# A gated hedgehog attention kernel: where the casts of the weight tails, one early weight split and four early stores stand in their engines' queues

## The chip, the cores and the metric

One core of a Trainium2 chip runs the whole kernel. Its engines work from queues of their own, each strictly in order: TensorE (PE, with its weight loads PEld), VectorE (DVE), ScalarE (ACT), GpSimd (POOL) and SyncE (SP), which here only issues transfers. Engines wait for one another, and for transfers, through semaphores. The metric is the time of one execution on the device, in microseconds (us).

## The reference

One row block of x (2048 rows, 576 columns, float32) goes through two branches whose results are joined:

```
xn = layernorm(x)
q, k, v = split of xn @ wqkv into 32 heads of 18
phi(t)  = [softmax(t @ w_phi), softmax(-t @ w_phi)]       for q and k, per head
o       = phi(q) (phi(k)^T v) / (phi(q) (phi(k)^T 1) + 1e-6)
s       = o @ wo
g       = silu( (silu(xn @ w_gate) * (xn @ w_up)) @ w_down )      4608 hidden columns
result  = x + s * g
```

## The kernel before

All products are float32-exact to a few bits by splitting each operand into a rounded part ("hi", type fp32r) and a rest ("lo"): ACT casts hi, DVE (or GpSimd) subtracts to get lo, and PE sums three products. So each operand costs one cast and one subtraction before PE can use it.

The work comes in five stages. *Preparation* (to about 70 us): x is loaded, normalised and transposed into eight blocks XB, and w_phi is folded into the weights of k and q. *Keys* (to about 230 us): sixteen key tiles of 128 rows, their softmaxes, and the sum kv = phi(k)^T v. *Queries* (to about 490 us): sixteen query tiles (`q_tile`), in pairs, with the numerator (`numer`) and the projection with wo (`project`) of the pair before. *Gate and up*, with *down*: 36 hidden blocks f of 128 columns in two row halves i, by a Strassen-like scheme that saves products. An end that joins the branches.

Five of the 36 hidden blocks, the early ones (`EARLY = 5`), are computed ahead, plainly, in the first three stages, as filling for PE: `early_weights(f)` (line 100) loads two raw weight pieces on SP's queue and splits each (`split_rows`: ACT's cast at line 62, DVE's subtractions at lines 63 and 64); `early_tile(f, i, parts)` (line 113) computes gate and up for two column groups of 512 rows, with a SiLU on ACT (line 119), a product on DVE (line 123), and a store of h to DRAM on SP's queue (line 124). The tiles of h have two buffers, and the two PSUM banks `pe` are shared by gate and up: the next gate product needs the SiLU of the one before to be done. The first two early blocks are done for the half i = 1 in the preparation (line 262); f = 1 and f = 0 are finished and f = 2, 3 done in the query stage (lines 645 to 648); f = 4 stands between the stages.

`tails(n)` (line 544) prepares, for four of the other hidden blocks at a time, the last 32 + 32 rows of the weights: a load on SP's queue (line 547), four subtractions on GpSimd (549 to 552), a cast on ACT (tile `th`, line 553), a subtraction on DVE (line 554), and twelve stores to DRAM issued by GpSimd (line 557): eight of the cast, four of the rest. There are eight of them, and the main stage reads what they store.

`softmax_parts` (line 275) is the part of a key or query tile behind its product: a maximum and a minimum over each head on DVE (line 280), two subtractions that read PSUM (line 281, kept in the list `read`, two a tile), two exponentials on ACT (line 284, the last of them kept in `exps`), and a sum. `q_tile` goes on with products on DVE, the last of which (line 580) is kept in `last_e`. There is one PSUM tile for the query product, so the next query tile's product (`p L92`) waits for the second subtraction of the tile before.

A planner lays out each engine's order: it takes instructions by their place in the program as they become ready by its own estimates, ahead of others where the code says `high_priority`. `tc.issue_after(ins)` binds it: what the block issues on the engine of `ins` stands behind `ins` in that engine's queue; instructions on other engines are not bound. So with `last_e[...]` around `tails(n)` (line 642), only the DVE subtraction of the tail is bound.

Of the kernel before, what the change touches and what calls it, by code (L numbers as in the profile page):

```python
# [18 lines left out]
NT = S // P  # L19
BT = 512  # L20
# [26 lines left out]
def gated_hedgehog_kernel(ctx: ExitStack, tc, x, w_qk, w_v, w_phi, wo, w_gu, w_tail, w_down, ident_in, mask_in, out):  # L47
# [5 lines left out]
    nc = tc.nc  # L53
# [7 lines left out]
    def split_rows(hi, lo, src):  # L61
        nc.scalar.copy(hi, src)
        nc.vector.tensor_sub(lo, src[:, :, 0:2], hi[:, :, 0:2])
        nc.vector.tensor_sub(hi[64:96, :, 2], src[64:96, :, 2], hi[64:96, :, 2])
# [6 lines left out]
    h_dram = dram.tile([2, EARLY, P, HS], F32, name="h_dram")  # L71
# [10 lines left out]
    def xw(ps, i, j, cols, wh, wl, stationary_x):  # L82
        pairs = []
        for k in range(2):
            b = XB[i][2 * j + k]
            for c in range(2):
                pairs += [(b[:, c, cols], w[:, k, c]) for w in (wh, wl)]
                pairs += [(b[:, 3 + c, cols], wh[:, k, c])]
            pairs += [(b[0:96, 2, cols], wh[0:96, k, 2])]
        for n, (a, b) in enumerate(pairs):  # L90
            l, r = (a, b) if stationary_x else (b, a)
            last = nc.tensor.matmul(ps, l, r, start=n == 0, stop=n == len(pairs) - 1)  # L92
        return last
# [3 lines left out]
    pes = ctx.enter_context(ExitStack())  # L97
    eps = pes.enter_context(tc.tile_pool(name="eps", bufs=2, space=PSUM, side="right"))

    def early_weights(f, behind=None):  # L100
        parts = []
        for m in (0, 2):
            raw = epool.tile([P, 2, 3, P], F32, name="raw", bufs=2)
            hi = epool.tile([P, 2, 3, P], F32R, name="wh", bufs=3)
            lo = epool.tile([P, 2, 2, P], F32R, name="wl", bufs=3)
            nc.sync.dma_start(raw, w_gu[f, :, m:m + 2])
            with tc.issue_after(behind.ins) if behind else ExitStack():
                with tc.high_priority():
                    split_rows(hi, lo, raw)
            parts.append((hi, lo))  # L110
        return parts

    def early_tile(f, i, parts, js=(0, 1), banks=None, behind=None):
        for j in js:
            pg, pu = banks or [eps.tile([P, BT], F32, name="pe") for _ in range(2)]
            xw(pg, i, j, slice(0, BT), *parts[0], False)
            h = epool.tile([P, BT], F32, name="h")
            with tc.high_priority():
                nc.scalar.activation(h, pg, AF.Silu)  # L119
            last = xw(pu, i, j, slice(0, BT), *parts[1], False)  # L120
            with tc.issue_after(behind.ins) if behind else ExitStack():
                with tc.high_priority():
                    nc.vector.tensor_mul(h, pu, h)
            nc.sync.dma_start(h_dram[i, f, :, j * BT:(j + 1) * BT], h)
        return last

    outs = []
    with ExitStack() as att:
# [9 lines left out]
        with ExitStack() as wst:  # L138
# [4 lines left out]
            with ExitStack() as pst:  # L143
# [91 lines left out]
                chain = norm_stats([2], xns[0:4])  # L235
                norm_block(2, xns[0:4])
                first_weights = [early_weights(0)]
                with tc.issue_after(chain.ins):
                    norm_stats([3], xns[4:8])
                fold(wk, KVWH[:, :, :, 0:D], KVWL[:, :, :, 0:D])  # L240
                norm_block(3, xns[4:8])
                first_weights.append(early_weights(1))
                wv = []
                for n in range(6):
# [14 lines left out]
                fold(wq, QH, QL)  # L259
                norm_block(1, xns[4:8])  # L260
                for f in range(2):
                    early_tile(f, 1, first_weights[f])

            pes.close()
            kt = wst.enter_context(tc.tile_pool(name="kt", bufs=1, reuse_waits="tile"))
# [25 lines left out]
            kk_pool, read, exps = kk, [], []  # L291
# [138 lines left out]
            order = [6, 7, 0, 1, 2, 3, 4, 5]  # L430
            for p in range(8):
# [56 lines left out]
                if p == 3:  # L488
                    keep_x()
            spare = early_tile(1, 0, first_weights[1], (0,), [kps.tile([P, BT], F32, name=n) for n in ("vy", "vx")])  # L490
            with tc.issue_after(spare.ins):
                kv_step(*pend)

        with ExitStack():
# [6 lines left out]
            banks = [(i, 4 if i < 2 else 2, GROUPS[2 * i][1]) for i in range(3)]  # L501
# [23 lines left out]
        with ExitStack() as qst:  # L525
# [15 lines left out]

            kk_pool = qk

            def tails(n):
                t = qk.tile([P, 7, P], F32, name="tl", bufs=2)
                hi = qk.tile([P, 7, P], F32R, name="th", bufs=1)
                nc.sync.dma_start(t[:, 0:4], w_tail[n])
                sub = nc.gpsimd.tensor_sub
                sub(t[:, 4], t[:, 2], t[:, 0])
                sub(t[:, 2], t[:, 3], t[:, 2])  # L550
                sub(t[:, 5], t[:, 3], t[:, 4])
                sub(t[:, 6], t[:, 1], t[:, 5])
                nc.scalar.copy(hi, t)
                nc.vector.tensor_sub(t, t, hi)
                for b, src in enumerate((hi.bitcast(F32), hi.bitcast(F32), t)):
                    for q in range(4):
                        nc.gpsimd.dma_start(t_dram[n, q, b], src[32 * q:32 * q + 32])
# [70 lines left out]
            order = list(range(S // QS // 2, S // QS)) + list(range(S // QS // 2))  # L628
# [11 lines left out]
                es = new  # L640
            for n in range(TAILS):
                with tc.issue_after(last_e[3 * n // 2 + 2].ins):
                    tails(n)

        for f, halves in [(1, (0,)), (0, (0,))] + [(f, (1, 0)) for f in range(2, EARLY - 1)]:
            parts = first_weights.pop() if f == 1 else early_weights(f, read[2 * NT + 1] if f == 0 else None)
            for i in halves:
                early_tile(f, i, parts, (1,) if f == 1 else (0, 1), behind=read[2 * NT + 1] if f == 1 else None)

# [76 lines left out]
    def stored(src, fill):  # L726
        h = h_tile()
        for r in range(2):
            nc.sync.dma_start(h[r], src[:, r * BT:(r + 1) * BT])
        for _ in range(2):  # L730
            fill()
        return h
# [267 lines left out]
    for i in range(2):  # L1000
        order = [NF - 1] * i + list(range(EARLY, NF - i))
# [27 lines left out]
    parts = early_weights(EARLY - 1)  # L1029
# [11 lines left out]
    for i, n, f in units:  # L1041
# [9 lines left out]
        h = stored(h_dram[i, f], fill) if f < EARLY else gate_up(w, xo, fill, f - EARLY + (NF if i else 0))  # L1051
# [60 lines left out]
```

## Time and profile before

| | |
|---|---|
| median of 3 runs | 1640.72 us (1638.78 to 1643.44) |
| the profiled execution | 1637.38 us |
| its span, first to last instruction | 1635.6 us |
| PE busy | 1605.0 us (98%) |
| DVE busy | 1167.2 us (71%) |
| ACT busy | 721.3 us (44%) |
| POOL busy | 655.4 us (40%) |
| mean granted PE clock | 0.996 |

A row of a timeline gives start, duration, engine, line, operation and operands, and in brackets the idle time of the engine just before it with what ended it. A row of the waits gives who waited for whom: us in total, times, longest. A row of the stretches gives each engine's busy time in a stretch, and what clock PE was granted in it (1.00 is full speed). The chain of waits follows back from the last instruction, at each step to what released it.

### The profile page before, as it was taken

The numbers are of one execution on the slowest core, as the hardware profiler recorded it, in microseconds if no ns is written. First come the engines' busy times: TensorE is split into PE (matmuls) and PEld (weight loads), VectorE is DVE, ScalarE is ACT, GpSimd is POOL, SyncE is SP. The second block draws the span as 40 slices with busy tenths as digits, with TensorE's granted clock in tenths as the row PEclk, the third lists the DMA queues.
The fourth block names the chain that finished last, engine by engine and source line by source line (L and its number), as shares of the span: only waits on it lengthen the run. The fifth ranks groups of instructions, "written<-read, shape, count | busy, mean of one in ns | idle before, by whom it ended". The sixth has DMA issues, their size and how long they took to land.

```text
span 1635.6 us, 25199 instructions
## 1 busy us (share of the span) xinstructions
PE 1605.0 (98%) x9385; PEld 1431.3 (88%) x9385; DVE 1167.2 (71%) x1721; ACT 721.3 (44%) x1391; POOL 655.4 (40%) x699
## 2 busy tenths in 40 slices
PE   6999998999999999999999999999999999999998
PEld 5899997999988888888888888888888888888887
DVE  7677768889863678778777778825676766666578
ACT  5533344454432554544444544455433333333334
POOL 3485661342302555455545355313233324133132
PEclk9999999999999999999999999999999999999999
DMA  8522243333329645554554454685454655556445
GB/s 287 205 80 78 88 137 112 117 110 95 97 86 326 227 165 169 175 188 160 182 177 164 174 195 152 220 300 149 136 168 130 200 184 172 170 179 184 140 115 174
DMA packets 121740, 268.46 MB, mean 164 GB/s; under 512 B 12786, under 2 KB 53362, under 8 KB 119826
## 3 DMA queue, kind: packets, MB, share of 16 engines
q1 hardware_dynamic: 106652, 246.49, 46.1%
q0 software_dynamic: 3072, 11.02, 2.5%
q10 hardware_dynamic: 11894, 9.35, 1.8%
q8 instruction: 74, 1.21, 0.3%
q14 instruction: 48, 0.39, 0.1%
HBM read 167.19 MB, written 99.61 MB: 163 GB/s over the span
## 4 chain that ended last, share of the span: by engine, by line
PE 92%; DMA 3%; DVE 2%; POOL 1%; ACT 1%; issue 1%; ACTq 0%; SPq 0%; POOLq 0%; DVEq 0%
PE px L713 24%; PE pd L838 24%; PE pw L713 12%; PE p L92 7%; PE py L713 6%; PE pe L92 6%; PE p L617 4%; PE kvp L297 2%; PE po L597 2%; PE vx L385 1%; PE pt L591 1%; PE vw L385 1%; DMA xn<-in_A_x 1%; PE tp L223 1%; DVE acc L810 0%
## 5 line engine op out<-in xcount | busy, mean ns | idle before, releaser
L838 PEld LDWEIGHTS pd<-dw,hh 128*128 128x128 f32 x3048 | 432.5, 189 | 23.2 <-ACT pd L859 1.5
L838 PE MATMUL pd<-dw,hh 128*128 128x288 f32 x3048 | 448.0, 297 | 1.7 <-ACT pd L859 0.7
L713 PE MATMUL px<-X,w 128*128 128x512 f32 x1488 | 384.5, 393 | 1.1 <-ACT s L742 1.0
L713 PEld LDWEIGHTS px<-X,w 128*128 128x128 f32 x1488 | 270.8, 188 | 53.1 <-ACT s L742 3.3
L713 PE MATMUL pw<-X,w 128*128 128x512 f32 x732 | 188.7, 393 | 0.0
L713 PEld LDWEIGHTS pw<-X,w 128*128 128x128 f32 x732 | 137.1, 189 | 30.3
L747 DVE TENSOR_TENSOR s<-pw,s 128x512 f32<-128x512 f32 x124 | 85.1, 687 | 101.1 <-ACT s L742 90.5
L963 DVE TENSOR_TENSOR acc<-pd,acc 128x576 f32<-128x576 f32 x128 | 96.2, 752 | 84.3 <-PE pd L838 84.2
L742 ACT COPY s<-px 128x512 f32<-128x512 f32 x124 | 72.6, 585 | 158.0 <-PE px L713 158.0
L92 PE MATMUL pe<-X,wh 128*128 128x512 f32 (+1 forms) x380 | 120.8, 401 | 5.6 <-ACT h L119 4.3
L59 DVE TENSOR_TENSOR hh<-ha,hh 128x512 fp32r<-128x512 f32 x140 | 108.6, 801 | 20.7 <-ACT hh L58 19.1
L58 ACT CAST hh<-ha 128x512 fp32r<-128x512 f32 x140 | 82.6, 619 | 92.1 <-PE pd L838 72.9
L935 POOL TENSOR_TENSOR hb<-hb 128x512 f32<-128x512 f32 x34 | 46.0, 1352 | 166.7 <-DVE hb L759 160.1
L59 DVE TENSOR_TENSOR w<-ld,w 128x512 fp32r<-128x512 f32 (+1 forms) x93 | 78.0, 841 | 35.9 <-ACT w L58 34.7
L713 PE MATMUL px<-X,wt 96*128 96x512 f32 x248 | 98.0, 395 | 0.0
L713 PE MATMUL py<-X,w 128*128 128x512 f32 x372 | 96.6, 394 | 0.6 <-ACT py L767 0.6
L922 POOL TENSOR_TENSOR h<-ha,hb 128x512 f32<-128x512 f32 x34 | 44.6, 1313 | 125.2 <-DVE ha L763 88.6
L948 POOL TENSOR_TENSOR ha<-ha 128x512 f32<-128x512 f32 x34 | 52.6, 1562 | 103.3 <-DVE hh L59 103.3
L58 ACT CAST w<-ld 128x512 fp32r<-128x512 f32 (+1 forms) x93 | 50.9, 549 | 88.0 <-POOL ld L703 56.7
L92 PEld LDWEIGHTS pe<-X,wh 128*128 128x128 f32 (+1 forms) x380 | 70.2, 190 | 20.1 <-ACT h L119 5.0
L767 ACT COPY py<-px 128x512 f32<-128x512 f32 x62 | 35.5, 572 | 102.7 <-PE px L713 80.8
L700 POOL TENSOR_TENSOR ts<-ld 128x256 f32<-128x256 f32 x31 | 26.9, 869 | 126.1 <-issue 70.9
(263 smaller groups left out, 3246.3 us busy)
## 6 DMA issues: line engine op xcount, KB each, us to landing
w_dram<-w SPq DMA_DIRECT2D x90, 512.0 KB, 2.9
w<-w_dram SPq DMA_DIRECT2D x90, 512.0 KB, 4.4
wt<-t_dram SPq DMA_DIRECT2D x61, 336.0 KB, 3.5
ld<-in_B_w_gu SPq DMA_DIRECT2D x31, 512.0 KB, 4.5
X<-sum_dram SPq DMA_DIRECT2D x8, 1280.0 KB, 12.4
rt<-in_B_w_down SPq DMA_DIRECT2D x33, 288.0 KB, 3.0
rb<-in_B_w_down SPq DMA_DIRECT2D x33, 288.0 KB, 5.0
w_dram<-w SPq DMA_DIRECT2D x30, 256.0 KB, 2.0
```

Of the source, the lines that this page charges most:

```text
L58: nc.scalar.copy(hi, src)
L59: nc.vector.tensor_sub(lo, src, hi)
L92: last = nc.tensor.matmul(ps, l, r, start=n == 0, stop=n == len(pairs) - 1)
L617: nc.tensor.matmul(ps[:, 0:HALF], a[0:w, g, jc], bw[0:w, g, n], start=k == 0, stop=k == 3 * NG - 1)
L713: nc.tensor.matmul(ps, l, r, start=first and n == 0, stop=last and n == len(mm) - 1, skip_group_check=True)
L742: nc.scalar.copy(t, ps)
L747: nc.vector.tensor_add(t, ps, t)
L838: nc.tensor.matmul(ps, l, r, start=first and n == 0 and m == 0, stop=n == len(hs) - 1 and m == 2, skip_group_check=True)
L922: sub(s, g["h"][0][0], g["h"][0][1])
L935: nc.gpsimd.tensor_add(a21, a21, g["h"][1][1])
L948: sub(a12, a12, g["h"][0][0])
L963: nc.vector.tensor_add(a2, pd[:, :, 0:HALF], a2)
```

## The change

Three things are moved; nothing is computed differently.

- `early_weights` takes any number of instructions to stand behind. For f = 2, the third early weights, both casts on ACT now stand behind the last exponential of the second query tile (`exps[NT + 1]`), and the subtractions on DVE behind its second subtraction (`read[2 * NT + 3]`). For f = 0 it stays as it was.
- In `tails(n)` the cast on ACT stands behind the last exponential of query tile 3n//2 + 2, the tile (from 0) whose last product the tail's DVE subtraction was bound to already.
- The stores of h of the four early tiles in the preparation (f = 0 and 1, i = 1, two each) are issued by GpSimd in place of SyncE.

```diff
-    def early_weights(f, behind=None):
+    def early_weights(f, *behind):
...
             nc.sync.dma_start(raw, w_gu[f, :, m:m + 2])
-            with tc.issue_after(behind.ins) if behind else ExitStack():
+            with ExitStack() as order:
+                for b in behind:
+                    order.enter_context(tc.issue_after(b.ins))
                 with tc.high_priority():
                     split_rows(hi, lo, raw)
...
-    def early_tile(f, i, parts, js=(0, 1), banks=None, behind=None):
+    def early_tile(f, i, parts, js=(0, 1), banks=None, store=nc.sync, behind=None):
...
-            nc.sync.dma_start(h_dram[i, f, :, j * BT:(j + 1) * BT], h)
+            store.dma_start(h_dram[i, f, :, j * BT:(j + 1) * BT], h)
...
-                    early_tile(f, 1, first_weights[f])
+                    early_tile(f, 1, first_weights[f], store=nc.gpsimd)
...
-            def tails(n):
+            def tails(n, behind):
...
-                nc.scalar.copy(hi, t)
+                with tc.issue_after(behind.ins):
+                    nc.scalar.copy(hi, t)
...
-                    tails(n)
+                    tails(n, exps[NT + 3 * n // 2 + 2])
...
-            parts = first_weights.pop() if f == 1 else early_weights(f, read[2 * NT + 1] if f == 0 else None)
+            parts = first_weights.pop() if f == 1 else early_weights(
+                f, *{0: read[2 * NT + 1:2 * NT + 2], 2: (read[2 * NT + 3], exps[NT + 1])}.get(f, ()))
```

## The prediction

> **What bounds the kernel now.** I read the busy times and the slices, then the busy time by stretch, then the list of who waited for whom on PE, then the chain of waits and the timeline around the one place that it points to.
>
> ```profile
> span 1635.6 us, 25199 instructions
> PE 1605.0 (98%) x9385; PEld 1431.3 (88%) x9385; DVE 1167.2 (71%) x1721; ACT 721.3 (44%) x1391; POOL 655.4 (40%) x699
> ```
> ```profile
> 0.00:60.00 60.00, 44.14 (x245) 36.59 (x246) 43.10 (x103) 35.12 (x48) 22.96 (x50) 1.00 0.87 293
> 240.00:262.00 22.00, 17.69 (x89) 15.12 (x88) 16.74 (x24) 10.04 (x11) 7.55 (x16) 0.84 0.67 205
> 262.00:480.00 218.00, 217.92 (x1447) 197.94 (x1445) 187.17 (x296) 97.05 (x170) 56.55 (x112) 1.00 0.31 90
> ```
> The second fence gives, for each stretch, busy time of PE, PEld, DVE, ACT and POOL, then the granted PE clock, the DMA share and GB/s. PE is the bound: 98% of the span. It can only win where it idles or runs slowly. The stretch from 262 to 480 is the query stage after its first two tiles; there PE idles 0.08 us in 218 us because matmuls of the early tiles are strewn between those of the queries. The only stretch with a lowered clock (0.84) is 240 to 262, and there PE also idles 4.31 us.
>
> ```profile
> PE tp L195 <- DVE xn L183: 12.6, 2, 10.8
> PE pe L92 <- ACT h L119: 4.3, 2, 4.1
> PE p L92 <- DVE e L281: 0.2, 1, 0.2
> ```
> Apart from the start (12.6 us on the first rows of x), the longest wait of PE is one of 4.1 us on the SiLU of an early tile. The chain of waits (start, us, what) tells why it was late, and has two rows that price PE's steps (the first and last):
>
> ```profile
> 71.22 3.73 PE p L92 x28
> ...
> 241.81 5.84 DMA tl<-in_B_w_tail
> ...
> 250.59 0.83 ACT wh L62
> ...
> 254.37 0.70 DVE e L281
> ...
> 255.21 5.52 PE p L92 x28
> ...
> 260.95 12.18 PE pe L92 x52
> ```
> The load of tail 0 (tl) ends at 247.65; GpSimd forms its differences; ACT casts it (th); behind that ACT casts the third early weights (wh, of f = 2); DVE splits them; only then come the second query tile's subtractions, which free its PSUM for the next 28 query matmuls. The timelines of ACT, DVE and PE there (start, us, idle before in brackets):
>
> ```profile
> 238.37 1.26 ACT L284 ACTIVATE e<-e 128x576 f32<-128x576 f32 x2
> 249.75 0.94 ACT L553 CAST th<-tl 128x896 fp32r<-128x896 f32 x1 [10.12 <-POOL tl L552]
> 252.73 0.60 ACT L119 ACTIVATE h<-pe 128x512 f32<-128x512 f32 x1
> ```
> ```profile
> 244.97 1.34 DVE L572 TENSOR_REDUCE y<-ez 128x64 f32<-128x1152 f32 x1
> 251.45 0.70 DVE L63 TENSOR_TENSOR wl<-raw,wh 128x512 fp32r<-128x512 f32 x1 [5.14 <-ACT wh L62]
> 252.16 0.42 DVE L64 TENSOR_TENSOR wh<-raw,wh 32x256 fp32r<-32x256 f32 x1
> 264.92 0.69 DVE L63 TENSOR_TENSOR wl<-raw,wh 128x512 fp32r<-128x512 f32 x1 [0.38 <-ACT wh L62]
> 266.85 0.69 DVE L123 TENSOR_TENSOR h<-pe,h 128x512 f32<-128x512 f32 x1 [1.24 <-PE pe L92]
> 267.76 0.69 DVE L63 TENSOR_TENSOR wl<-raw,wh 128x512 fp32r<-128x512 f32 x1 [0.22 <-ACT wh L62]
> 271.85 0.75 DVE L281 TENSOR_TENSOR e<-p,m 128x576 f32<-128x576 f32 x1
> ```
> ```profile
> 253.38 0.79 PE L92 MATMUL pe<-X,wh 128*128 128x512 f32 x1 [4.12 <-ACT h L119]
> ```
> ACT stands idle 10.12 us in front of th, with a SiLU behind it whose input is done; DVE stands 5.14 us in front of wl with the query's work behind it. PE runs out of what it may do at 249.26.
>
> **Term 1, the stall.** The tail's cast goes behind the third query tile's exponential and the weights' cast and split behind the second tile's. Then ACT's next work after 239.63 is the SiLU. Its 14 matmuls are the first half of the 28 that end at 249.26; at 12.18/52 = 0.234 us each they are done near 245.9, so the SiLU is done near 246.6 (0.60), before PE needs the bank. DVE goes on at 244.97 + 1.34 = 246.31. Before, from the start of the split (251.45) to the end of the second subtraction (254.37 + 0.70) it took 3.62 us; so it frees the PSUM at 249.93 at the latest, and 0.69 + 0.42 = 1.1 us earlier if the split comes after, near 248.8, and PE asks at 249.26 + 3 x 0.234 = 249.96. So the 4.12 us go whole.
>
> **Term 2, the clock.** The windows after the stall, same columns as above:
>
> ```profile
> 253.40:255.30 1.90, 1.71 (x4) 0.93 (x4) 1.90 (x6) 1.89 (x3) 1.90 (x5) 0.50 0.90 141
> 255.30:258.30 3.00, 3.00 (x13) 3.00 (x14) 2.97 (x5) 3.00 (x5) 0.34 (x1) 0.50 0.98 376
> ```
> The granted clock is 0.50 for about 5 us after the gap. The 28 query matmuls took 5.52 us against 3.73 in the first chain row: 1.79 lost. The three early ones took 255.21 - 253.38 = 1.83 against 0.70: 1.13 lost, its 0.19 us of waiting among it. Together 2.92. Without the gap there is no reason for it. The Trainium skill (TensorE: Matmul & The Clock Gate, "What's actually happening") has the clock halved after an idle window of about 3.4 us and restored after about 3.4 us of work; the trace agrees with the half (0.50 after 4.12 us idle), and by the page's length alone this term would be an estimated 1.7 us and the sum 6 us, but the measured 5 us at 0.50 decide.
>
> Terms 1 and 2: -7.04 us. **What is late next.** PE comes 7.04 us earlier, DVE 5.14 at first. Before the third tile's subtraction (ends 272.60, PE's next query matmul 273.13) DVE idles 0.38 + 1.24 + 0.22 = 1.84 us for work that PE and ACT bring and that now comes earlier, so it regains 6.98 of the 7.04: 0. In the rest of the query stage DVE has 31 us free in 218.
>
> **Term 3, the tails' other casts.** For tail n the cast goes behind tile 3n//2 + 2. Six of the eight casts stand there already. Tail 0's goes from 249.75 to behind the third tile's exponentials, which follow its subtraction (272.60 in the old time), and tail 4's, now ahead of tile 8's exponentials, by some 16 us too:
>
> ```profile
> 351.35 0.94 ACT L553 CAST th<-tl 128x896 fp32r<-128x896 f32 x1
> ...
> 366.20 1.26 ACT L284 ACTIVATE e<-e 128x576 f32<-128x576 f32 x2
> ```
> Eight stores on POOL's queue go with each cast; POOL is idle there (56.55 busy of 218) and the next thing in its queue is the same tail's rest, which waits for DVE behind the tile's last product anyway. The main stage alone reads the tails. On ACT 0.94 us is put between an exponential and the numerator's casts, with ACT at 97.05 of 218: 0, hidden by the 52 early matmuls of the chain's last row. If that cover is gone, 0.94 each, 1.9 in all.
>
> The third weights are next needed after those 52, half of them other tiles': about 260 in the new time, and their cast can follow the second tile's exponential, near 250: 0, with some 8 us to spare.
>
> **Term 4, the four stores.** They leave SP's queue (in order) for POOL's (in order too).
>
> ```profile
> 37.11 0.69 DVE L123 TENSOR_TENSOR h<-pe,h 128x512 f32<-128x512 f32 x1
> ...
> 52.80 0.69 DVE L123 TENSOR_TENSOR h<-pe,h 128x512 f32<-128x512 f32 x1 [0.75 <-ACT h L119]
> ```
> ```profile
> 38.47 8.65 SPq L213 DMA_DIRECT2D wst<-in_A_w_qk  x4
> 47.17 0.90 SPq L124 DMA_DIRECT2D h_dram<-h  x2
> ```
> ```profile
> PE pe L92 <- ACT h L119: 0.2, 1, 0.2
> ```
> ```profile
> 50.88 1.28 ACT L119 ACT_TABLE_LOAD   x1 [1.82 <-DMA h_dram<-h]
> ```
> ```profile
> 39.75 2.51 POOL L205 TENSOR_TENSOR X<-xr,X 32x512 fp32r<-32x512 f32 x2 [2.33 <-ACT xr L203]
> 50.72 2.67 POOL L186 COPY xn<-xn 128x128 f32<-128x128 f32 x8 [6.56 <-DVE xn L183]
> ```
> ```profile
> L557 POOL DMA_DIRECT2D t_dram<-th x64: 496/496/658, 251.5 to 431.1; - x64
> ```
> The first store is ready at 37.80 and goes at 47.17, behind four weight loads that wait for buffers; its landing lets ACT take the third SiLU, which waited 1.82 us. That gain is real on ACT, but of PE's waits in the first 60 us only 0.2 are for ACT's SiLU (the row of waits above): at most 0.2. Cost: the trace has no 128-row store from POOL; the 32-row one issues in 0.496 us, so 0.5 to 2.0 (four times the rows) each, 2 to 8 us of a POOL that is busy 22.96 of 60. In front of L205 POOL idles 2.33 us, so the first store hides there. The range is -0.2 to +3 (see rival 3), I take 0. SP's later loads only come earlier. A rule against: the Trainium skill (SBUF — State Buffer, "SBUF: two separate sides") says that GpSimd cannot write its DMA descriptors while VectorE holds the shared port. Here 64 issues with DVE 86% busy took at most 0.658 us, 0.16 over the median, so by the trace it costs under 1 us for four.
>
> **Sum.** -7.04 + 0 + 0 + 0 = -7.0 us. The profiled execution took 1637.4 us (span 1635.6 and 1.8 around it) and would take 1630.4; the median shown is 3.3 us higher, 1640.7, and becomes 1633.7.
>
> **The rivals.** About 0.3%, 4.9 us, is what a measurement of this kernel can tell from no change.
>
> 1. *DVE becomes the late one.* If DVE does not regain the 1.84 us, because the planner puts the splits of f = 2 and 3 ahead of the third tile's reductions, PE waits at that tile: 7.04 - 5.14 = 1.90, less the 0.53 between 272.60 and 273.13, and 1.1 for a split more: 2.5 us, 1636.2. For it speaks that DVE is at 86% (187.17 of 218), against it that PE waited for DVE only 0.2 us in this stage.
>
> 2. *Slower: DVE waits in its queue for the moved casts.* A tail's subtraction stands on DVE behind the tile's last product; with the cast no longer made long ahead, it can wait for ACT, and ACT can stand in front of a projection's copy:
>
> ```profile
> ACT so L625 <- PE p L617: 45.1, 27, 2.6
> ```
> So 2.6 + 0.94 = 3.5 us of DVE, at tails 0 and 4. It decides only if PE has no early matmuls left there, so that PE idles too and the clock falls again: 2 x (3.5 + 2.9) = 12.8, less 7.0: +5.8, 1646.5. Against it: the six casts that already stand so hold DVE up in no row of its waits.
>
> 3. *POOL's queue holds x up.* The transposes at stake:
>
> ```profile
> 53.87 2.46 PE L195 MATMUL tp<-ident,xn 128*128 128x128 f32 x21
> ```
>
> If the third store (ready at 52.80 + 0.69 = 53.5) is queued ahead of the copies at 50.72, the transposes of those copies, the last eight of this row, at about 55.3, wait for eight copies of 2.67/8 = 0.33 us after 53.5 + 2.0: until 58.2, about +3 us: 1636.7.
>
> 4. *It doesn't do what it says.* Another late cast takes the place in front of the SiLU (the output weights' casts are bound behind the same exponential, so not they): 1640.7.
>
> **How the numbers follow.** Forecast 0.60, rival 1 0.15, rival 2 0.15, rivals 3 and 4 0.05 each. Faster by over 0.3% is the forecast alone, 0.60; rivals 1, 3 and 4 lie within 0.3%, 0.25; slower 0.15. The forecast's own range is 1630 to 1636: 1.9 us of run to run below and half of term 1 above. The range for all goes from 1630 to 1643, over rivals 1, 3, 4 and a mild form of rival 2.
>
> **What would show it.** Term 1: no th or wh between the first query tile's exponentials and the next SiLU on ACT, and no 4.1 us of PE behind L119. Term 2: clock 1.00 from 240 to 262. Term 3: eight casts each behind their tile's exponentials, no DVE wait on th. Term 4: h stores on POOL of 0.5 to 2 us, ACT's 1.82 us gone, PE's idle in the first 60 us within 0.3 of 15.9. It is wrong if PE idles over 1 us between 245 and 480.

## The result, and the profile after

The changed kernel takes 1632.16 us (median of 6 runs, 1631.01 to 1633.36) against 1640.16 us (6 runs, 1638.68 to 1643.44) before on the same chip: a ratio of 0.9951, 95% interval 0.9938 to 0.9964. The prediction was 1633.7 us. Run again on another chip (below), the change gave 0.9962 (0.9948 to 0.9976). The profiled execution took 1633.12 us, its span is 1631.0, 4.6 us below the 1635.6 of before.

The busy times by stretch of the changed kernel, columns as in the prediction:

```profile
0.00:60.00 60.00, 44.43 (x240) 37.58 (x241) 43.69 (x103) 35.38 (x48) 24.13 (x53) 0.97 0.89 293
240.00:262.00 22.00, 21.76 (x118) 18.78 (x117) 21.80 (x32) 11.50 (x14) 5.10 (x8) 1.00 0.51 163
```

In the stretch from 240 to 262 PE is busy 21.76 us instead of 17.69, and its granted clock is 1.00 instead of 0.84. What ACT does there (timeline of the changed kernel):

```profile
238.78 1.26 ACT L286 ACTIVATE e<-e 128x576 f32<-128x576 f32 x2
...
246.42 0.60 ACT L121 ACTIVATE h<-pe 128x512 f32<-128x512 f32 x1 [5.08 <-PE pe L92]
...
250.45 0.84 ACT L62 CAST wh<-raw 128x768 fp32r<-128x768 f32 x1 [0.78 <-DMA raw<-in_B_w_gu]
...
269.50 0.94 ACT L556 CAST th<-tl 128x896 fp32r<-128x896 f32 x1
```

The SiLU (L121, was L119) comes 6.3 us earlier than before, as soon as PE has given it its product. One row holds something the prediction did not have: the third weights' cast, now behind the second tile's exponential, still waits 0.78 us for its own load, which lands only at about 250.4. So not one load but two came after the time at which the SiLU was ready to go. The experiments begin there.

PE's rows at the borders of the query stage, its first product and the first gate-up product, of before and then of after:

```profile
228.45 0.38 PE L92 MATMUL p<-QH,X 128*128 128x288 f32 x1
512.74 1.53 PE L713 MATMUL px<-X,w 128*128 128x512 f32 x6
```
```profile
228.85 0.38 PE L92 MATMUL p<-QH,X 128*128 128x288 f32 x1
506.44 1.54 PE L717 MATMUL px<-X,w 128*128 128x512 f32 x6
```

From the first row to the second is the query stage: 284.29 us before, 277.59 after, 6.70 less. From the second row to the end of the span is the rest: 1122.86 before, 1124.56 after, 1.70 more. The preparation differs by 0.40. So -6.70 + 1.70 + 0.40 = -4.6. The 0.40 holds a stretch at half clock (granted 0.50) that this execution has near 20 us and the one of before has not: the same 36 products that fold w_phi into the weights took 5.91 us behind a wait of 2.07, in place of 4.28 behind one of 1.41 (PE's rows, before and then after):

```profile
17.77 4.28 PE L223 MATMUL tp<-PHI,wst 126*128 126x126 f32 x36 [1.41 <-DVE X L198]
```
```profile
18.50 5.91 PE L225 MATMUL tp<-PHI,wst 126*128 126x126 f32 x36 [2.07 <-DVE X L200]
```

The same three lengths of every profiled kernel below come from the same two rows of its timeline and its span:

| kernel | before the queries | query stage | rest | span |
|---|---|---|---|---|
| before | 228.45 | 284.29 | 1122.86 | 1635.6 |
| after | 228.85 | 277.59 | 1124.56 | 1631.0 |
| after, run again | 227.34 | 277.28 | 1124.48 | 1629.1 |
| e1 both bindings, no stores | 228.75 | 277.61 | 1124.94 | 1631.3 |
| e2 stores alone | 226.95 | 283.70 | 1122.95 | 1633.6 |
| e3 tails' binding alone | 227.41 | 285.66 | 1123.23 | 1636.3 |
| e4 third weights' binding alone | 231.82 | 282.42 | 1124.56 | 1638.8 |
| e5 tail load early | 229.23 | 278.60 | 1121.67 | 1629.5 |
| e6 tail 0's cast alone | 229.23 | 277.58 | 1124.49 | 1631.3 |
| e7 gate-up order | 228.49 | 277.77 | 1123.54 | 1629.8 |
| e8 gate-up order, second form | 229.81 | 277.73 | 1122.26 | 1629.8 |
| e9 second load late | 226.78 | 277.67 | 1124.95 | 1629.4 |

The first column varies by 5 us, for kernels that do the same there as well as for those that don't. Half clock in the preparation is part of that: the executions of after, e4, e6, e7 and e8 have such a stretch (3.4 us, in e4 6.8) and took 229.64 us there on average, the other seven have none and took 227.84. It comes with the stores on either engine. The other two columns stay within 0.6 us for kernels whose order there is the same. They are the better ruler here.

Where the 1.70 us go shows in the first 21 us from the first gate-up product. PE idles 0.04 us in them before and 2.49 after:

```profile
512.74:533.74 21.00, 20.96 (x91) 16.90 (x90) 12.36 (x18) 10.04 (x20) 8.26 (x9) 1.00 0.84 292
```
```profile
506.44:527.44 21.00, 18.51 (x80) 14.54 (x79) 12.07 (x18) 9.51 (x20) 10.27 (x12) 1.00 0.75 257
```

The 2.49 us are two waits (who waits for whom on PE, changed kernel):

```profile
PE px L717 <- ACT s L746: 1.4, 1, 1.4
PE px L717 <- ACT py L771: 1.1, 1, 1.1
```

Before, PE has a wait of each kind too, of 1.0 and 0.6, but later. From there to the end it idles 0.81 us less after than before (8.47 against 9.28), so PE's idle time makes 1.64 of the 1.70.

### The profile page after: what moved, and what is told of

Read it like the earlier page. It is cut to its first block, busy times and chain, and to the rows that moved or that the text cites. A ratio compares the mean times of both kernels' runs of the same rounds, so it can differ in the third digit from the quotient of the medians.

```text
span 1631.0 us, 25196 instructions
## 1 busy us (share of the span) xinstructions
PE 1602.5 (98%) x9385; PEld 1429.8 (88%) x9385; DVE 1172.8 (72%) x1721; ACT 722.4 (44%) x1391; POOL 654.7 (40%) x703
## 4 chain that ended last, share of the span: by engine, by line
PE 93%; DVE 3%; DMA 2%; ACT 1%; issue 1%; POOL 0%; SPq 0%; ACTq 0%; DVEq 0%; POOLq 0%
PE pd L842 24%; PE px L717 24%; PE pw L717 12%; PE p L92 7%; PE pe L92 6%; PE py L717 6%; PE p L620 4%; PE kvp L299 2%; PE po L600 2%; PE vx L387 1%; PE pt L594 1%; PE vw L387 1%; DMA ld<-in_B_w_gu 1%; PE vy L92 1%; PE vx L92 1%
```

## Experiments: which part carries the gain

Theory 1 was that of the prediction: tail 0's load is late, its cast holds ACT, and the third weights are behind it. Theory 2, from the row at 250.45: both loads are late, and either cast alone, ahead of the SiLU, holds it for some 4 us, so neither binding is worth much without the other. Four kernels ran on one chip beside 27 runs of before (median 1638.05 us).

**e1: both bindings, the stores back on SyncE.**

```diff
-                    early_tile(f, 1, first_weights[f], store=nc.gpsimd)
+                    early_tile(f, 1, first_weights[f])
```

> The two bindings (tails' casts, third weights) without the stores, which stay on SyncE. Theory (the stores are worth nothing on PE): the whole gain, 8.0 us of the changed kernel, so about 1632; PE not idle behind the early SiLU near 249, clock 1.00 from 240 to 262, ACT's wait of 1.8 us for h's store near 50 back. Rival (the stores carry the part of the gain above the predicted 7 us): 1 us slower than the changed kernel, 1633.

Measured: 1633.15 us, ratio 0.9967 (0.9955 to 0.9980). The two bindings carry the change: query stage and rest are those of the changed kernel within 0.4 us. The time is the rival's 1633, but before is faster here as well (1638.05 against 1640.16), and the interval overlaps that of the change (0.9938 to 0.9964), so these runs cannot tell whether the stores add anything to the bindings. The change was therefore run again (below).

**e2: the stores alone, both bindings undone.**

```diff
-                with tc.issue_after(behind.ins):
-                    nc.scalar.copy(hi, t)
+                nc.scalar.copy(hi, t)
...
-                f, *{0: read[2 * NT + 1:2 * NT + 2], 2: (read[2 * NT + 3], exps[NT + 1])}.get(f, ()))
+                f, *{0: read[2 * NT + 1:2 * NT + 2]}.get(f, ()))
```

> Only the four stores on GpSimd, no binding. Theory: no change, 1640 within 0.5 us; PE idles 4.1 us behind the early SiLU near 249 as before, with the clock at 0.50 after it. Rival (the stores matter by themselves): faster by 1 us, 1639, or, if POOL's queue holds x up, slower by up to 3 us, 1643.

Measured: 1638.43 us, ratio 0.9996 (0.9987 to 1.0005): nothing. GpSimd's timeline has the four stores:

```profile
37.25 0.72 POOL L126 DMA_DIRECT2D h_dram<-h  x1 [0.69 <-DVE h L125]
46.28 0.56 POOL L126 DMA_DIRECT2D h_dram<-h  x1 [2.82 <-DVE h L125]
52.58 0.54 POOL L126 DMA_DIRECT2D h_dram<-h  x1 [0.24 <-DVE h L125]
72.47 0.57 POOL L126 DMA_DIRECT2D h_dram<-h  x1
```

Together 2.39 us of GpSimd, as they came ready, and PE's wait behind the SiLU is there as before (4.42 us).

**e3: the tails' binding alone.** Only the third weights' binding (the last diff of e2) and the stores are undone.

> Only the tails' casts bound; the third weights' cast stands ahead of the SiLU as before. Theory 1 (the prediction's reading: the tail's cast, waiting for its load, is what is late, the weights' cast only stands behind it): ACT casts wh from about 247, the SiLU is done by 250, DVE frees the PSUM near 251.5; PE idles under 2 us, the clock holds, 1635. Theory 2 (formed from the changed kernel, whose cast of these weights still waited for their load until 250.4: both loads are late, either alone holds the SiLU): wh is cast at 250.4, the SiLU done near 253, PE idles 3.9 us, the clock falls, gain under 0.5 us: 1640.

Measured: 1639.35 us, ratio 1.0001 (0.9992 to 1.0010). ACT's and PE's timelines:

```profile
249.83 0.83 ACT L62 CAST wh<-raw 128x768 fp32r<-128x768 f32 x1 [11.23 <-DMA raw<-in_B_w_gu]
...
251.97 0.60 ACT L121 ACTIVATE h<-pe 128x512 f32<-128x512 f32 x1
```
```profile
252.62 0.51 PE L92 MATMUL pe<-X,wh 128*128 128x512 f32 x1 [4.40 <-ACT h L121]
```

Tail 0's cast is out of the way, and ACT stands 11.23 us for the other load instead. PE waits as long as before. Theory 1 alone falls here.

**e4: the third weights' binding alone.** The tails' binding (the first diff of e2) and the stores are undone.

> Only the third weights bound; the tail's cast stands ahead of the SiLU as before. Theory 1: th is cast at 249.75 as before, then the SiLU without the 0.8 us of the weights' cast, done near 252.6: PE idles 3.3 us in place of 4.1. If the clock still falls: gain 0.8, 1639.3. If a gap of 3.3 us is too short for it to fall: gain 0.8 + 2.7, 1636.7. Theory 2 says the same for this kernel; DVE, no longer behind the weights' split, frees the PSUM for the query in time.

Measured: 1639.32 us, ratio 1.0004 (0.9995 to 1.0014). ACT and PE:

```profile
253.33 0.94 ACT L555 CAST th<-tl 128x896 fp32r<-128x896 f32 x1 [10.32 <-POOL tl L554]
...
255.58 0.60 ACT L121 ACTIVATE h<-pe 128x512 f32<-128x512 f32 x1
```
```profile
263.21 0.50 PE L92 MATMUL pe<-X,wh 128*128 128x512 f32 x1 [2.91 <-DVE h L125]
```

Now it is the tail's load again that holds the SiLU, and behind it the second tile's exponentials. PE's wait comes later and elsewhere: it waits 2.91 us for DVE's product h, which stands in DVE's queue behind the sum over those exponentials (4.28 us of waiting) and the split of the third weights. The clock fell, so of the two cases the smaller gain was to be expected. The query stage is 1.87 us shorter than before, and the rest is 1.70 longer. Theory 2 holds: the gain is there only with both. DVE was in time for the query's PSUM, as it said, but late with this product.

## Experiments: why the tail's cast was late, and whether its place matters

These three ran on another chip beside 12 runs of before (median 1639.68 us).

**The change again.**

> The kernel after once more, beside the runs that follow. The two bindings alone took 1633.15 us against 1638.05 before (ratio 0.9967). If the four stores on GpSimd carry nothing, as term 4 has it and as their own run says (0.9996), this comes out at a ratio of 0.995 to 0.998 with a preparation that differs from run to run by a microsecond or two. If the stores are worth something beside the bindings that they are not worth alone, it comes out below 0.995, over 2 us faster than the two bindings, and its first key matmul starts earlier than at 71.4 us.

Measured: 1632.46 us, ratio 0.9962 (0.9948 to 0.9976), overlapping that of e1 (0.9967) almost wholly. No worth of the stores beyond the bindings can be told.

**e5: tail 0's and 1's loads ahead of those of the output weights.**

```diff
+            tl_first = [qk.tile([P, 7, P], F32, name="tl", bufs=2) for _ in range(2)]
+            for n, t in enumerate(tl_first):
+                nc.sync.dma_start(t[:, 0:4], w_tail[n])
...
-                nc.sync.dma_start(t[:, 0:4], w_tail[n])
+                if n > 1:
+                    nc.sync.dma_start(t[:, 0:4], w_tail[n])
...
-                with tc.issue_after(behind.ins):
+                with tc.issue_after(exps[NT].ins):
...
-                    early_tile(f, 1, first_weights[f], store=nc.gpsimd)
+                    early_tile(f, 1, first_weights[f])
```

> Third weights bound as in the change and stores on SyncE; the tails' casts are not bound behind their tile, only (all of them) behind the first query tile's last exponential, and the loads of tails 0 and 1 are issued on SyncE ahead of those of the output weights. Theory (late load): tail 0's cast held the SiLU in the run with the third weights bound alone because its load, behind five others in a stretch with the DMA queues 67% to 98% busy, landed at about 247.6 us. Issued ahead it lands some 4 us earlier, near 244; the cast is over by about 247 and the SiLU by about 249, so PE's wait of 4.1 us shrinks to under 1, the clock stays at 1.00 in 240 to 262, and the time falls 4 to 7 us: ratio 0.9957 to 0.9976. Rival (the place on ACT is what counts, not the load): the cast stands ahead of the SiLU as before, PE waits 3 us or more there at a clock of about 0.85, and the time is within 1.5 us of before: ratio 0.999 to 1.001.

Measured: 1632.49 us, ratio 0.9960 (0.9945 to 0.9974). GpSimd, ACT and PE:

```profile
243.28 0.46 POOL L555 TENSOR_TENSOR tl<-tl 128x128 f32<-128x128 f32 x1 [4.81 <-DMA tl<-in_B_w_tail]
```
```profile
246.48 0.95 ACT L560 CAST th<-tl 128x896 fp32r<-128x896 f32 x1 [6.07 <-POOL tl L558]
...
250.15 0.60 ACT L121 ACTIVATE h<-pe 128x512 f32<-128x512 f32 x1
```
```profile
250.05 0.37 PE L92 MATMUL p<-QH,X 128*128 128x288 f32 x1 [1.88 <-DVE e L283]
```

The load lands 4.5 us earlier than before (GpSimd began at 247.8 there) and the gain stays, with the cast ahead of the SiLU. So what has to go is a late input at the head of ACT's queue, and it can go by moving the load as well as by moving the cast. Two details were off: the SiLU was done at 250.75, 1.8 us later than expected, since ACT took an exponential of the second tile (248.16, 0.68) ahead of it, and PE waited 1.88 us there, not under 1, for the second tile's subtraction. The query stage is 1.0 us longer than the changed kernel's and the rest 2.9 shorter (1121.67): this kernel has no give-back (next section).

**e6: of the tails' casts only tail 0's is bound.**

```diff
-                with tc.issue_after(behind.ins):
+                with tc.issue_after(behind.ins) if n == 0 else ExitStack():
```

> The change with tail 0's cast alone bound behind its tile; the other seven are left to the planner. By term 3 of the prediction the other bindings are worth nothing: same time as the change within 1 us, ratio 0.996 to 0.998, PE idle under 1.5 us in 262 to 480. If tail 4's cast behind tile 8 was part of the gain, or another tail's cast now goes early and holds an exponential or a SiLU up, PE waits over 1 us somewhere between 262 and 480 and this is 1 to 4 us slower than the change.

Measured: 1633.05 us, ratio 0.9959 (0.9946 to 0.9971), the same. Tail 4's cast goes early, and nothing waits for that (ACT's timeline, and PE's busy time in the rest of the query stage):

```profile
344.44 0.95 ACT L556 CAST th<-tl 128x896 fp32r<-128x896 f32 x1
```
```profile
262.00:480.00 218.00, 217.13 (x1463) 197.94 (x1462) 185.38 (x293) 98.05 (x174) 60.06 (x123) 1.00 0.33 101
```

In the changed kernel the same cast stands at 357.67.

## Experiments: the 1.7 us given back

In the changed kernel SyncE issues the two loads for the second pair's preparation (rt and rb) together, ahead of the loads of h; before, they were 6.4 us apart. GpSimd then takes that preparation (td) ahead of the last weight difference (ld) that PE's products want, and ACT a cast of it ahead of a copy. SyncE's rows of before and of after, and GpSimd's of after:

```profile
521.14 0.33 SPq L896 DMA_DIRECT2D rt<-in_B_w_down  x1
...
527.53 0.42 SPq L896 DMA_DIRECT2D rb<-in_B_w_down  x1
```
```profile
509.80 0.47 SPq L900 DMA_DIRECT2D rt<-in_B_w_down  x1
510.33 0.47 SPq L900 DMA_DIRECT2D rb<-in_B_w_down  x1
```
```profile
516.27 0.80 POOL L927 TENSOR_TENSOR td<-rb,rt 128x288 f32<-128x288 f32 x1
517.15 0.81 POOL L932 TENSOR_TENSOR rt<-rt 128x288 f32<-128x288 f32 x1
518.04 0.81 POOL L933 TENSOR_TENSOR td<-rb,rt 128x288 f32<-128x288 f32 x1
519.48 0.74 POOL L707 TENSOR_TENSOR ld<-ld,ts 128x256 f32<-128x256 f32 x1 [0.63 <-DVE w L59]
```

**e7: GpSimd's part of the second pair's preparation behind the weight differences.**

```diff
+    sums_done = []
...
-            nc.gpsimd.tensor_sub(ld[:, 1], ld[:, 1], ts[:, 1])
+            sums_done.append(nc.gpsimd.tensor_sub(ld[:, 1], ld[:, 1], ts[:, 1]))
...
-                    h, w = f(g)
+                    with tc.issue_after(sums_done[2].ins) if first and i == 0 and n else ExitStack():
+                        h, w = f(g)
```

> The change, and GpSimd's part of the preparation of the second pair of combined weights (first pass, second item on) is held behind the weight differences of the gate-up stage's third block. It is meant for the 1.7 us that the change gives back behind the query stage, where the changed kernel's trace has GpSimd do that preparation (516.3 to 518.9 us) ahead of the differences at 519.5 and PE then waits 1.1 and 1.4 us at the first gate-up products. If GpSimd's order is the cause: PE busy in 520 to 560 rises from 36.95 to 38 or more, the stretch from the first gate-up product to the end goes from 1124.6 back to about 1122.9, and the kernel is 1 to 2 us faster than the change, ratio to before 0.9945 to 0.9965. If the cause is elsewhere (ACT's casts or the load itself): the same waits at the same size, same time as the change within 0.7 us, or slower where the held preparation is late for its own products.

Measured (same chip as e5 and e6): 1631.57 us, ratio 0.9949 (0.9937 to 0.9962); the rest 1123.54, 1.0 shorter where 1.7 was expected, and PE busy 37.92 us in 520 to 560 where 38 or more was. The time cannot be told from the change's (0.9962 beside it, intervals overlapping); the gain is read from the trace. The wait for py is gone, the one for s (1.50 us) is not, and ACT's timeline says why:

```profile
524.17 0.43 ACT L58 CAST dw<-td 128x288 fp32r<-128x288 f32 x1 [3.75 <-POOL td L936]
524.51 0.61 ACT L58 CAST w<-ts 128x512 fp32r<-128x512 f32 x1
525.03 0.58 ACT L748 COPY s<-px 128x512 f32<-128x512 f32 x1
```

It is the picture of the query stage again, smaller: a cast whose input is late, with a copy that PE wants queued behind it.

**e8 and e9** ran on the chip of e1 to e4, beside 9 runs of before (median 1638.60 us). e8 moves the three differences of the fourth product a block further; e9 leaves GpSimd alone and holds the load of rb on SyncE.

```diff
-                    with tc.issue_after(sums_done[2].ins) if first and i == 0 and n else ExitStack():
+                    with tc.issue_after(sums_done[2 + part].ins) if first and i == 0 and n else ExitStack():
```

> As the run before, but of the second pair's preparation GpSimd's first difference alone (for the seventh product) stands behind the third gate-up block's weight differences, and the three of the fourth product stand a block later. In the run before, one of the two waits went (1.1 us on the copy into py) and one stayed (1.5 us on the copy s), behind ACT's cast of the fourth product's weights, which stood 3.75 us idle for GpSimd. Theory (ACT's cast in front of the copy is the cause): the 1.5 us goes too, the stretch from the first gate-up product to the end is 1121.5 to 1122.9, and the ratio to before is 0.993 to 0.995. Rival (the cast only moves its wait to the next block's copy into py, which now stands behind it): a wait of 1 to 1.5 us at a later product, and the time is that of the run before, 0.9945 to 0.9965.

Measured: 1629.94 us, ratio 0.9951 (0.9938 to 0.9963); the rest 1122.26, 2.2 to 2.3 us shorter than the change's. From the first gate-up product PE's timeline has no wait until one of 0.56 us, so the rival's new wait did not come either:

```profile
507.54 1.54 PE L719 MATMUL px<-X,w 128*128 128x512 f32 x6
...
534.48 0.53 PE L844 MATMUL pd<-dw,hh 128*128 128x288 f32 x2 [0.56 <-ACT hh L58]
```

```diff
+    w_stores = []
...
-                    nc.sync.dma_start(w_dram[f - EARLY, :, m:m + k], w.bitcast(F32))
+                    w_stores.append(nc.sync.dma_start(w_dram[f - EARLY, :, m:m + k], w.bitcast(F32)))
...
-                    g["bottom"] = down_rows(g["f"][1], "rb")
+                    with tc.issue_after(w_stores[8].ins) if first and i == 0 else ExitStack():
+                        g["bottom"] = down_rows(g["f"][1], "rb")
```

> The change, and nothing but the load of the second pair's lower rows (rb, on SyncE) held behind the first weight store of the third gate-up block, near where SyncE issues it in the kernel before (527.5 us, 6.4 behind rt; in the changed kernel 510.3, 0.5 behind rt). If the early load is what lets GpSimd and ACT take the preparation too early: no wait of 1 us or more at the products between 505 and 535 us, the stretch from the first gate-up product to the end 1121.5 to 1122.9, ratio 0.993 to 0.995. If the preparation then comes too late for its own products (its casts stand behind those of four more on ACT): a new wait of PE at pd near 540 us of 1 us or more, and a ratio of 0.9955 or above.

Measured: 1631.55 us, ratio 0.9954 (0.9941 to 0.9968); the rest 1124.95, no gain. The waits between 505 and 530 are gone here too. But up to 533.3 ACT stands 3.19 us for a sum that GpSimd does behind its now late preparation, then 1.75 us for the last part of that preparation, and PE pays it, in wait and in clock, at a copy queued behind these casts (pd was expected):

```profile
539.06 2.33 PE L719 MATMUL px<-X,w 128*128 128x512 f32 x6 [2.07 <-ACT s L748]
```
```profile
539.85:543.15 3.30, 3.30 (x12) 2.85 (x11) 2.83 (x4) 1.47 (x4) 1.47 (x2) 0.50 0.98 326
```

e9 moved more than it was meant to: the third pair's rt went up as well, from 535 to 508 us. So it shows that a late load takes these two waits away, and not what the load of rb alone is worth. In the traces, putting the preparation at the right place in GpSimd's and ACT's queues (e8) recovers 2.2 us; with it too late (e9) nothing is left of the gain. Query stage and rest of e8 together take 1399.99 us, 7.16 less than before, and those of e5, where the loads stand apart, 6.88 less: near the 7.04 of terms 1 and 2, as expected where nothing is given back. e8 has the lowest median of all, yet its ratio cannot be told from the change's (0.9951 and 0.9962, intervals overlapping): that it beats the change rests on its trace, not on the times.

## Why the prediction was right, and where it was not

**Terms 1 and 2** said -7.04 us: 4.12 of stall and 2.92 of slow clock. The query stage became 6.70 us shorter (6.52 to 7.01 in the run again, e1, e6, e7, e8 and e9, which put both casts behind the exponentials too). PE's idle time in 240 to 262 went from 4.31 to 0.24 and the clock from 0.84 to 1.00, so both parts went whole there. Over the whole query stage PE idles 3.38 us less (5.40 to 2.02) and is busy 3.32 us less (278.89 to 275.57). Of the idle time that came in anew, most is one wait that was not there before:

```profile
486.46 0.50 PE L92 MATMUL pe<-X,wh 128*128 128x512 f32 x1 [0.71 <-ACT h L121]
```

The cause inside term 1 was half of it. The prediction had one late load, the tail's, with the third weights queued behind its cast. e3 shows the third weights' own load as late as the tail's. The sum came out right only because the change binds both.

**What is late next** was put at 0. For DVE that was right: rival 1 (1636.2 us) asked for a wait at the third tile's subtraction, and PE has none there: from 240 to 480 us it waits for DVE once, 0.24 us, for another product (at 251.65). But the prediction looked for the next late thing only as far as the query stage went. The step that failed is this 0: the planner's order at the start of the gate-up stage changed along with it, GpSimd and ACT took a later pair's preparation first, and 1.70 us were given back, a term that the sum does not have. e4, with one binding and no gain, has rt and rb together too, two such waits (1.3 and 1.1) and the same rest (1124.56); e2, e3 and e5 have the loads some 6 us apart and a rest of 1121.67 to 1123.23. So it goes with the planned order, not with PE coming earlier.

**Term 3**, the tails' other casts, 0: right (e6). Rival 2, DVE waiting in its queue for the casts of tails 0 and 4, did not come: no row has DVE waiting for th, and PE idles 1.06 us in 262 to 480, 1.02 of it the wait for ACT's copy at line 628, which before (1.01, line 625) stood just behind the end of that stretch. The sign that was to prove the prediction wrong, over 1 us idle between 245 and 480, thus appeared for a reason that has nothing to do with it: the bound was put in fixed times although the work was to move by 7 us.

**Term 4**, the stores, 0: right (e2, and e1 beside the change). The price was put at 0.5 to 2.0 us each; a store of 128 rows took 0.54 to 0.72, little more than the 0.496 of 32 rows, so the upper end, four times the rows at four times the price, was far too high. ACT's wait of 1.82 us for the first store went (the table load ahead of its SiLU follows at 50.42 without a wait). PE's idle time in the first 60 us went from 15.86 to 15.57, within the 0.3 that was said, but it says little: the half clock near 20 us stretches PE's busy time there. Rival 3 did not come: the third store went at 54.48 between the copies, and PE idles no more than before in those 60 us in e2 and in the run again either (15.15 and 15.27, at full clock).

**Rival 4**, that another late cast takes the place ahead of the SiLU, did not happen in the change, but e3 is exactly this case, and its 1.0001 is what the rival said.

**The number.** 1633.7 was taken as the median minus 7.0; 1632.16 came out. That it came so near is luck in part: the give-back of 1.70 was missing, and the traces show 4.6 to 6.5 us of difference in span (1635.6 against 1631.0 and 1629.1) where the first pair of medians shows 8.0. The stages behind the preparation account for 5.0 to 5.4 us (query stage and rest together, 1407.15 before, 1402.15 and 1401.76 after). The medians of before lay 2.8 us above its profiled execution (1640.16 and 1637.4), that of after 1.0 below its own. Part of the rest has a row: the half clock near 20 us, which lost 1.63 us (5.91 against 4.28) in the profiled execution of after and did not occur in that of before. For the executions without a profile it stays open what varied.

## What to carry to other kernels

A cast that waits for its load at the head of an in-order queue holds everything behind it; look for every such input that lands late, since taking away only one shows the other at much the same price (ratios 1.0001 and 1.0004 for either binding alone, 0.9967 for both). It can be cured at the load or at the place in the queue. After a binding has been added, read the start of the next stage too: the planned order can move there, and a preparation made too early cost as much here as one made too late (the rest took 1124.56 and 1124.95 us, against 1122.26 with it in place).

## What the runs showed of the hardware

Half clock comes in whole windows of 3.41 us. Stretches with PE's granted clock at 0.50 in before and in e4 (start:end, length, then busy times and the clock as above); that of e9 is shown already:

```profile
251.80:258.70 6.90, 5.14 (x18) 4.35 (x19) 6.82 (x14) 6.84 (x9) 3.83 (x8) 0.51 0.77 227
```
```profile
263.90:267.40 3.50, 3.50 (x10) 2.75 (x9) 3.50 (x6) 0.89 (x2) 0.00 (x0) 0.51 0.21 78
```

After waits of 4.12 us (before), 4.42 (e2), 4.40 (e3) and 3.05 (the first of e4's two) the low clock lasted two windows, part of the first while PE still stood idle; after 2.91 (e4's second), 2.48 (e6), 2.25 (e8) and 2.07 us (e9, after) it lasted one, and in e4's second and e9 it began 0.7 to 0.8 us after PE had started again.

The length of the wait alone does not decide. The windows stand on a grid that runs on through the execution: e4's two stretches begin at 18.20 and 263.96 us, and the 245.76 between them are 72 times 3.413. What counts is how long PE idles within one window of the grid. e4's windows ahead of its two stretches, then a wait of 1.88 us in e5 that lies across a border, then one of 1.85 us in e7 that lies within a window, with the window behind it:

```profile
14.79:18.20 3.41, 1.22 (x11) 0.98 (x9) 1.14 (x3) 3.23 (x5) 0.00 (x0) 1.00 1.03 347
260.55:263.96 3.41, 0.75 (x3) 0.66 (x4) 3.37 (x5) 3.38 (x4) 0.00 (x0) 1.00 0.64 195
```
```profile
248.53:251.94 3.41, 1.89 (x14) 1.90 (x15) 3.21 (x6) 3.36 (x4) 3.41 (x8) 1.00 0.97 337
251.94:255.36 3.42, 3.42 (x24) 3.19 (x23) 2.53 (x4) 3.41 (x5) 0.46 (x1) 1.00 0.40 135
```
```profile
30.29:33.71 3.42, 1.57 (x10) 1.07 (x9) 3.31 (x9) 2.87 (x5) 0.57 (x2) 1.00 1.04 280
33.71:37.12 3.41, 3.41 (x17) 2.99 (x16) 3.13 (x9) 1.16 (x2) 3.41 (x9) 0.50 0.91 295
```

PE idles 2.19 and 2.66 us in e4's two windows, 1.52 in e5's and 1.85 in e7's. In the twelve traces, laid out on the grid from the first record of the clock on, half clock followed every window at full clock with 1.86 us or more of idle time and none with 1.6 or less; between, both occur (1.85 us in before left the clock at 1.00). A second window at half clock followed where PE still idled 0.86 us or more in the first (1.73 in before, 0.86 in e4), and full clock where it idled 0.2 or less.

The Trainium skill (TensorE: Matmul & The Clock Gate, "What's actually happening") has a free-running window of about 3.4 us in which activity is judged; the lengths and the grid agree with it. It names an idle window as the condition; here a wait of 2.07 us, well short of a window, was enough. So a stall of 2 us on PE cost about 1.7 us more in clock (half of e9's 3.41; 1.63 in the row of after at 18.50), and one of 4 us 2.9 by term 2's two rows.
